# Reordering attention around the first feed-forward phases of a fused attention and feed-forward kernel on one core

## The chip, the core and the metric

The kernel runs on one core of one Trainium2 chip. The metric is the device time of one execution in microseconds (us); lower is better. Times are told as the median of several runs. A profile of one execution has its own span, from the first to the last instruction.

The engines named here: TensorE (PE in the profile, its weight loads PEld) multiplies matrices into the eight banks of PSUM; VectorE (DVE) and ScalarE (ACT) work on tensors; GpSimd (POOL) here only issues loads, and SyncE (SP) only issues stores and a few small loads. A suffix q (SPq, ACTq) stands for an instruction of an engine's queue, such as issuing a DMA.

## The reference

Eight batches of eight heads, 512 local and 32 global positions of 64 numbers a head:

```python
s_g = scale * np.matmul(q_g, k_all.transpose(0, 1, 3, 2))
out_g = np.matmul(sm(s_g), v_all)
mask = np.abs(pos[:, None] - pos[None, :]) <= 32
s_ll = np.where(mask, scale * np.matmul(q_l, k_l.transpose(0, 1, 3, 2)), -1e9)
s_lg = scale * np.matmul(q_l, k_g.transpose(0, 1, 3, 2))
out_l = np.matmul(sm(np.concatenate([s_lg, s_ll], -1)), np.concatenate([v_g, v_l], 2))
...
x = attn_out.transpose(0, 2, 1, 3).reshape(B * S, H * D)      # 4352 x 512
h = x @ w_in                                                  # 512 -> 2048
return (h * (1 / (1 + np.exp(-1.702 * h)))) @ w_out           # 2048 -> 512
```

So global queries look at everything, local queries at the global keys and a band of 32 to each side, and the result goes through a feed-forward layer with a quick GELU. The inputs are float32; the kernel multiplies in bf16.

## The kernel before, in words

**Attention, by quads.** A `Quad` is four heads of one batch, so each batch has two, called `a` and `c` in the code, and quads 0 to 15 follow each other. The four heads lie on the four groups of 32 partitions. A quad goes through these steps:

- `Tk`, `Tq` (together `T`, L254 to L268): VectorE turns keys and queries, 128x512 each; `ext` (L270): four small copies put the global queries beside the local ones. `transpose_g` (L208) turns the global queries and keys of a batch.
- `S(rnd)` (L277): TensorE makes the scores of one half (round 0 or 1) of the key chunks, 16 matmuls for the four heads into four banks of PSUM (`s4`, one buffer). A score tile has two chunks of columns beside each other, 228 and 200 wide (200 and 228 in round 0). Quad 0's second half goes to four single banks instead.
- `X(rnd)` (L314): ScalarE takes the exponential of the whole tile in one instruction, 128x1712, or bank by bank for quad 0's second half. `M(rnd)` (L325): VectorE multiplies by the band mask, 128x1408.
- `gg` and `K` (L350, L330): scores of global keys; `XK` (L354) their exponential; `eg` (L336) a block-diagonal copy.
- `ekU(unit)` (L358) and `U(unit)` (L378): TensorE adds, in one bank per unit (`ov`), the part of the global keys and that of the local keys: unit 0 is the sums of the softmax, units 1 and 2 are the two halves of the values. `UG` and `ekUs` call these in order.
- `R` (L408): VectorE turns the sums, takes the reciprocal and turns it back; `XL(0)`, `XL(1)` (L418) scale units 1 and 2 into `xL`, the input of the feed-forward layer. `Gm` (L393) and `G` (L421) do the same for the global queries (the result goes to `xG`).

**Feed-forward, by batches.** For each batch i, an h phase of 16 steps (`h_step`, L466): four matmuls of 512 columns into one bank (`hp`), ScalarE's tanh (L462) and VectorE's product (L463) into `gT`. Then an o phase: four tiles of 128 rows, each of four o steps (`o_mm`, L473) of four matmuls; the last step of a tile calls `o_out` (L485): ScalarE copies the bank to `ob`, and four stores go out, issued by SyncE. The global rows of all batches are one more pass at the end (i = B); its last tile is computed by columns in two parts, each with its own copy and stores.

**What sets the order.** Each engine does its instructions in the order in which the Python code issues them; that order is written out by hand. Attention of batch i + 1 is placed inside the o phase of batch i (`phase_o`, L672) and, for the first quad of it, near the end of the phase before. The first phases are written out step by step: quads 0 and 1 at L511 to L589, the h phase of batch 0 at L591, its o phase with quads 2 and 3 at L608 to L650 (`osteps(0, (tile, quarter), ...)` are its o steps), and the h phase of batch 1 at L655 to L670, with the preparation of quad 4, the first of batch 2, put in after certain steps. Waits between engines are set by the framework from the tiles that an instruction reads and writes. The four banks of the pool `psP` are shared by `hp`, `op`, `ov`, `kb` and `og`, each taking one as it comes free.

**Loads.** GpSimd issues keys, queries, values and the weights in one fixed order (`load_rest`, L214): values of batch 0, four blocks of w_in, two of w_out, then the rest. Block 1 of w_in covers the first half of d_model for the first half of d_ff, block 2 the second half of d_model, blocks 3 and 4 the same for the other half of d_ff.

**Dummies.** `keep(n, ps)` (L160) issues n matmuls on a tile of zeros; 62 of them stand at the beginning, four more before the second scores of quad 0.

Of the kernel before, what the change touches and what calls it, by code (L numbers as in the profile page):

```python
# [15 lines left out]
AF = mybir.ActivationFunctionType  # L16
# [4 lines left out]
def kernel(  # L21
# [12 lines left out]
    nc = tc.nc  # L34
# [9 lines left out]
    scale = 1.0 / (D ** 0.5)  # L44
# [5 lines left out]
    LW = 352  # L50
    RW = 428
# [105 lines left out]
    warm = consts.tile([128, 512], BF16)  # L157
    nc.vector.memset(warm, 0.0)

    def keep(n, ps, w=512):  # L160
        for _ in range(n):
            nc.tensor.matmul(ps[:, :w], lhsT=warm[:, 0:128], rhs=warm[:, :w], start=True, stop=True)
# [12 lines left out]
    mask = consts.tile([128, 2, LW], BF16)  # L175
# [32 lines left out]
    def transpose_g(lo, hi, names="qk"):  # L208
        for name, dst, s in (("q", qgT, rqg), ("k", kgT, rkg)):
            if name not in names:  # L210
                continue
            nc.vector.transpose(dst[:, lo:hi, :32], s[:, lo:hi].bitcast(F32))
# [21 lines left out]
    def pbank(name):  # L234
        return psP.tile([128, 512], F32, name=name, tag="p")

    class Quad:
# [73 lines left out]
                                     rhs=rv[:, :, ee] if len(rv.shape) == 3 else rv[:, :, :, ee],  # L311
                                     start=(ee == 0), stop=(ee == 1), skip_group_check=True)

        def X(self, rnd):  # L314
            e = self.E[rnd]
            if isinstance(self.ps, list):
                for j in range(4):
                    n = RW + 32 if j == 2 else RW
                    nc.scalar.activation(e[:, j, :n], self.ps[j][:, :n], AF.Exp, scale=scale)  # L319
                return  # L320
            nc.scalar.activation(e[:, :, :RW], self.ps[:, :, :RW], AF.Exp, scale=scale)  # L321
            if rnd == self.gr:
                nc.scalar.activation(e[:, 2, RW:], self.ps[:, 2, RW : RW + 32], AF.Exp, scale=scale)

        def M(self, rnd):  # L325
            lo = 36 if rnd else 40
            e = self.E[rnd][:, :, lo : lo + LW]
            nc.vector.tensor_mul(e, e, mask[:, rnd : rnd + 1, :].to_broadcast([128, 4, LW]))  # L328

        def K(self, e=None):  # L330
            if e != 1:
# [23 lines left out]
            self.ek = att.tile([128, Sl], BF16, name="ek")  # L355
            nc.scalar.activation(self.ek, self.kb, AF.Exp, scale=scale)  # L356

        def ekU(self, unit):  # L358
            ov = self.st[unit] = pbank("ov")
            for j in range(4):  # L360
                r = 32 * ((j + 1) % 4)
                p = slice(r, r + 32)
                lv = (ones32[p] if unit == 0 else
                      rvg[p, self.Q, :D].rearrange("p (w h) -> p w h", h=2)[:, :, unit - 1])
                nc.tensor.matmul(ov[32 * j : 32 * j + 32, :], lhsT=lv, rhs=self.ek[p],  # L365
                                 start=True, stop=False, skip_group_check=True)
# [99 lines left out]
    def h_step(i, fc):  # L466
        if fc == 0:
            gTs[i] = moe.tile([128, FC, TB], BF16, name="gT")
        hp = pbank("hp")
        h_mm(i, fc, hp, range(NKC))  # L470
        h_act(i, fc, hp)

    def o_mm(i, st):  # L473
        tci, f4 = divmod(st, 4)
        first = (i, tci) not in ops
        if first:
            ops[i, tci] = pbank("op")
        op = ops[i, tci]
        for fc in range(4 * f4, 4 * f4 + 4):
            nc.tensor.matmul(op, lhsT=gTs[i][:, fc, tci * 128 : tci * 128 + 128],  # L480
                             rhs=w_out_sb[:, fc, :], start=(first and fc == 4 * f4), stop=(fc == FC - 1))
        if f4 == 3:
            o_out(i, tci, op)

    def o_out(i, tci, op):  # L485
        ob = moe.tile([128, d_model], F32, name="ob", bufs=6)
        last = i == B and tci == B // 4 - 1
        for lo, hi in ((0, 256), (256, 512)) if last else ((0, 512),):
            if last:
                op = pbank("op")  # L490
                for fc in range(FC):
                    nc.tensor.matmul(op[:, lo:hi], lhsT=gTs[i][:, fc, tci * 128 : tci * 128 + 128],  # L492
                                     rhs=w_out_sb[:, fc, lo:hi], start=(fc == 0), stop=(fc == FC - 1))
            nc.scalar.activation(ob[:, lo:hi], op[:, lo:hi], AF.Copy, scale=0.5)  # L494
            for j in range(4):
                eng = nc.scalar if lo and j % 2 else nc.sync
                if i < B:
                    rows = out[i * S + Sg : (i + 1) * S, :].rearrange("(r t) m -> t r m", t=16)[4 * tci + j]
                else:
                    r = (4 * tci + j) * S  # L500
                    rows = out[r : r + Sg, :]
                eng.dma_start(out=rows[:, lo:hi], in_=ob[32 * j : 32 * j + 32, lo:hi])
# [8 lines left out]
    a, c = Quad(0), Quad(1)  # L511
# [37 lines left out]
    c.K(0)  # L549
    a.ekU(0)  # L550
    c.K(1)
    a.ekU(1)
    a.ekU(2)
    c.XK()
    a.U(0)
    a.R()
    c.S(1)
    c.X(1)
    a.U(1)
    a.U(2)  # L560
    a.Gm()
    c.M(0)
    a.XL(0)
    c.M(1)
    a.XL(1)
    gTs[0] = moe.tile([128, FC, TB], BF16, name="gT")
    pt = pts[0] = psS.tile([128, 4, 512], F32, name="s4")
# [36 lines left out]
    def osteps(i, *sts):  # L604
        for tci, f4 in sts:
            o_mm(i, 4 * tci + f4)

    nq = {1: (Quad(2), Quad(3)), 2: (Quad(4), Quad(5))}  # L608
    a, c = nq[1]
    a.T()  # L610
    a.ext()
    osteps(0, (0, 1), (0, 0), (1, 1), (1, 0))
    c.ext()
    a.S(0)
    a.gg()
# [2 lines left out]
    a.XK()  # L618
    a.M(0)
    a.eg()  # L620
    osteps(0, (2, 1), (2, 0), (0, 2), (0, 3))
    a.S(1)
    a.X(1)
    c.T()
    a.M(1)
    osteps(0, (1, 2), (1, 3))
    osteps(0, (2, 2))
    c.S(0)
    osteps(0, (2, 3))
    a.ekUs(c)  # L630
    c.XK()
    c.X(0)
# [4 lines left out]
    a.U(2)  # L637
    c.S(1)
    a.Gm()
    a.XL(0)  # L640
    a.XL(1)
    a.G()
    c.M(0)
    c.eg()
    c.X(1)
    c.M(1)
    osteps(0, (3, 1), (3, 2))
    c.UG()
    c.RXG()
    osteps(0, (3, 3))  # L650
    a, c = nq[2]
# [2 lines left out]
    load_g(8, NQ)  # L654
    for fc in range(FC):  # L655
        h_step(1, fc)
        if fc == 3:
            a.T()
        if fc == 5:
            transpose_g(4, 6)  # L660
            a.ext()
        if fc == 7:
            a.S(0)
            a.gg()
            a.K()
            a.XK()
            a.X(0)
        if fc == 10:
            a.M(0)
            a.eg()  # L670

# [66 lines left out]
    for st in range(4):  # L738
        o_mm(B, st)
    o_out(B, 1, None)  # L740


# [28 lines left out]
```

## Time and profile before

| | |
|---|---|
| median of 6 runs | 315.32 us (314.39 to 316.2) |
| the profiled execution: its own time | 315.11 us |
| its span, first to last instruction | 313.4 us |
| TensorE busy | 299.0 us (95%) |
| VectorE busy | 210.8 us (67%) |
| ScalarE busy | 167.2 us (53%) |
| GpSimd busy | 80.0 us (26%) |
| first h matmul of batch 0 / of batch 1 | 19.8 us / 58.7 us |
| first scores after the h phase of batch 1 | 75.1 us |
| last o matmul ends / last store is issued | 309.5 us / 310.7 us |

A row of the timeline has the start in us, the duration in us, the engine, the line of the kernel, the operation, output and inputs with their sizes, the count, and in brackets how long the engine had been idle and what ended that. A row with a count above 1 covers several instructions in a row. Busy time of TensorE overlaps from one matmul to the next, so the duration of one matmul is longer than the spacing between two.

### The profile page before, as it was taken

Reading aid. Unit: us, or ns where it says so; the run is one execution under the profiler, and the core shown is the slowest. Engines: PE = TensorE matmul, PEld = TensorE weight load, DVE = VectorE, ACT = ScalarE, POOL = GpSimd, SP = SyncE. Lnnn points to the kernel's source line nnn. Section 1 sums busy time; section 2 is a strip of 40 time slices with the busy share of each in tenths; the row PEclk is TensorE's granted clock in tenths of the full one; section 3 lists DMA queues with packets and bytes.
Section 4 is the critical chain, followed back from the end, with each engine's and each line's share of the span. In section 5 each row is a group of like instructions: output and inputs, shape, how many; then the busy total and the mean of one; then the engine's idle time right before and its main releaser. Section 6 shows DMA issues by size and latency. Waiting matters only on the chain.

```text
span 313.4 us, 7832 instructions
## 1 busy us (share of the span) xinstructions
PE 299.0 (95%) x3214; PEld 148.6 (47%) x3250; DVE 210.8 (67%) x462; ACT 167.2 (53%) x253; POOL 80.0 (26%) x131
## 2 busy tenths in 40 slices
PE   7779999989999999999999999999999999999994
PEld 7334444434454454544554454444454444446653
DVE  7887945869767766777867866776857865474320
ACT  4816565366455654566536744565456642563421
POOL 8821578787018000720036000300000000000000
PEclk9999999999999999999999999999999999999999
DMA  7999999999939411990259212900211012201122
GB/s 155 146 189 207 207 137 198 179 160 147 93 72 167 68 27 44 118 152 2 46 83 168 46 36 64 108 0 19 52 41 30 0 38 50 52 0 28 41 64 71
DMA packets 60099, 27.44 MB, mean 88 GB/s; under 512 B 43296, under 2 KB 51744, under 8 KB 60064
## 3 DMA queue, kind: packets, MB, share of 16 engines
q0 software_dynamic: 51536, 17.11, 50.4%
q1 hardware_dynamic: 8000, 9.18, 12.0%
q10 hardware_dynamic: 528, 0.66, 0.6%
q8 instruction: 25, 0.41, 0.5%
q14 instruction: 10, 0.08, 0.1%
HBM read 35.13 MB, written 8.91 MB: 141 GB/s over the span
## 4 chain that ended last, share of the span: by engine, by line
PE 82%; DVE 5%; DMA 4%; POOL 4%; issue 2%; ACT 2%; DVEq 0%; POOLq 0%; ACTq 0%
PE op L480 35%; PE hp L455 31%; PE s L291 5%; PE ov L387 4%; DMA w_in_sb<-in_moe_w_in_dram 4%; PE ov L365 2%; POOL rk L84 2%; DVE gT L463 1%; PE op L492 1%; POOL v L97 1%; DVE e L328 1%; PE kb L310 1%; ACT th L462 1%; DMA rk<-in_k_l_dram 1%; DVE xL L419 1%
## 5 line engine op out<-in xcount | busy, mean ns | idle before, releaser
L480 PE MATMUL op<-w_out_sb,gT 128*128 128x512 bf16 x503 | 119.8, 380 | 1.8 <-issue 0.8
L463 DVE SCALAR_TENSOR_TENSOR gT<-th,hp 128x512 bf16<-128x512 f32 (+1 forms) x140 | 91.2, 656 | 43.1 <-ACT th L462 42.5
L455 PE MATMUL hp<-xL,w_in_sb 128*128 128x512 bf16 x487 | 108.1, 379 | 0.8 <-DVE gT L463 0.2
L462 ACT ACTIVATE th<-hp 128x512 f32<-128x512 f32 (+1 forms) x140 | 79.9, 573 | 43.5 <-PE hp L455 39.9
L455 PEld LDWEIGHTS <-w_in_sb 128*128 128x128 bf16 x576 | 56.1, 98 | 66.5 <-DMA w_in_sb<-in_moe_w_in_dram 1.6
L480 PEld LDWEIGHTS <-gT 128*128 128x128 bf16 x528 | 49.1, 98 | 56.2 <-issue 3.5
L321 ACT ACTIVATE e<-s 128x1712 bf16<-128x1712 f32 x31 | 49.5, 1597 | 14.3 <-PE s L404 8.9
L494 ACT ACTIVATE ob<-op 128x512 f32<-128x512 f32 (+1 forms) x35 | 20.5, 585 | 64.5 <-PE op L480 62.0
L97 POOL DMA_DIRECT2D v<-in_v_l_dram x36 | 27.0, 760 | 99.3 <-PE s L404 93.0
L84 POOL DMA_DIRECT2D rk<-in_k_l_dram x64 | 34.8, 553 | 11.9 <-DMA w_in_sb<-in_moe_w_in_dram 5.8
L410 DVE STREAM_TRANSPOSE sT<-ov 128x512 f32<-128x512 f32 x16 | 11.5, 717 | 33.1 <-PE ov L387 33.1
L328 DVE TENSOR_TENSOR e<-e,mask 128x1408 bf16<-128x1408 bf16 x32 | 28.0, 874 | 5.8 <-ACT e L321 5.5
L291 PE MATMUL s<-q,kT 32*128 32x200 bf16 (+1 forms) x512 | 21.3, 284 | 2.4 <-DVE q L273 0.7
L419 DVE TENSOR_TENSOR xL<-ov,rs 128x512 bf16<-128x512 f32 x32 | 20.7, 686 | 1.5
L291 PEld LDWEIGHTS <-kT 32*128 32x128 bf16 x512 | 11.1, 95 | 15.5 <-issue 10.0
L387 PE MATMUL ov<-e,v 128*32 128x192 bf16 (+1 forms) x512 | 13.1, 239 | 0.8 <-DMA v<-in_v_l_dram 0.8
L356 ACT ACTIVATE ek<-kb 128x512 bf16<-128x512 f32 x16 | 9.6, 600 | 8.1 <-PE kb L310 8.0
L414 DVE STREAM_TRANSPOSE rs<-rT 128x512 f32<-128x512 f32 x16 | 11.4, 712 | 0.6
L260 DVE STREAM_TRANSPOSE kT<-rk 128x512 f32<-128x512 f32 (+1 forms) x17 | 11.4, 673 | 0.2 <-DMA rk<-in_k_l_dram 0.2
L263 DVE STREAM_TRANSPOSE q<-rq 128x512 f32<-128x512 f32 (+1 forms) x17 | 10.9, 645 | 0.6 <-DMA rq<-in_q_l_dram 0.6
L387 PEld LDWEIGHTS <-v 128*32 128x32 bf16 x512 | 9.8, 96 | 2.9 <-issue 2.9
L310 PE MATMUL kb<-q,kgT 32*32 32x512 bf16 x128 | 10.0, 385 | 0.5 <-ACT e L319 0.5
(70 smaller groups left out, 153.5 us busy)
## 6 DMA issues: line engine op xcount, KB each, us to landing
out_dram<-ob SPq DMA_DIRECT2D x132, 64.0 KB, 1.8
rk<-in_k_l_dram POOLq DMA_DIRECT2D x64, 64.0 KB, 3.9
v<-in_v_l_dram POOLq DMA_DIRECT2D x28, 128.0 KB, 4.3
rq<-in_q_l_dram POOLq DMA_DIRECT2D x6, 512.0 KB, 6.9
w_in_sb<-in_moe_w_in_dram POOLq DMA_DIRECT2D x4, 512.0 KB, 12.6
w_out_sb<-in_moe_w_out_dram POOLq DMA_DIRECT2D x4, 512.0 KB, 13.8
rq<-in_q_l_dram POOLq DMA_DIRECT2D x3, 256.0 KB, 8.0
q<-in_q_l_dram ACTq DMA_DIRECT2D x1, 512.0 KB, 4.7
```

The source lines that it names most:

```text
L84: nc.gpsimd.dma_start(out=loaded[b][0][32 * j : 32 * j + 32, u], in_=kf[b, j][:, u])
L97: nc.gpsimd.dma_start(out=vtiles[b % 2][p, s, :, :, :D], in_=vf[b, t][:, hs])
L291: nc.tensor.matmul(ps[j][:, off : off + n * nr], lhsT=self.k[p, 128 * c : 128 * c + 128, e], rhs=self.q[p, t0 : t0 + n, r0 : r0 + nr, e], ...
L321: nc.scalar.activation(e[:, :, :RW], self.ps[:, :, :RW], AF.Exp, scale=scale)
L328: nc.vector.tensor_mul(e, e, mask[:, rnd : rnd + 1, :].to_broadcast([128, 4, LW]))
L387: nc.tensor.matmul(ov[32 * j : 32 * j + 32, :].rearrange("p (t r) -> p t r", t=16)[:, :, r0 : r0 + nr], lhsT=lv, rhs=self.E[c // 2][:, j, ...
L419: nc.vector.tensor_mul(self.x[:, 2 * self.u + h, :], self.st[1 + h], self.st["rs"])
L455: nc.tensor.matmul(hp[:, : width(i)], lhsT=w_in_c[:, fc // 8, kc, fc % 8 // 2, :, fc % 2], rhs=(xL[i] if i < B else xG)[:, kc, :], start=( ...
L462: nc.scalar.activation(th[:, :n], hp[:, :n], AF.Tanh, scale=0.851)
L463: nc.vector.scalar_tensor_tensor(gTs[i][:, fc, :n], in0=th[:, :n], scalar=1.0, in1=hp[:, :n], op0=ALU.add, op1=ALU.mult)
L480: nc.tensor.matmul(op, lhsT=gTs[i][:, fc, tci * 128 : tci * 128 + 128], rhs=w_out_sb[:, fc, :], start=(first and fc == 4 * f4), stop=(fc = ...
L494: nc.scalar.activation(ob[:, lo:hi], op[:, lo:hi], AF.Copy, scale=0.5)
```

## The change

The diff touches six places.

1. `ekU` gets dummies of its own: before it adds the part of the global keys, it can issue `warm` matmuls on zeros into its bank. In quad 0, units 1 and 2 of it move behind the sums and their transposes, with 3 and 4 dummies; unit 2 comes after the second scores of quad 1.
2. The second exponential of quad 1 (the last scores of batch 0) is done in two pieces, one per chunk of keys, and its mask in two pieces as well (192 and 160 columns a head).
3. In the o phase of batch 0, the o step (2, 1) moves ahead of quad 2's scores, and (2, 3) ahead of quad 3's.
4. In the same phase, VectorE's steps of quads 2 and 3 are ordered anew: quad 3's first mask ahead of quad 2's scaling, its second mask next, then `eg`, and quad 2's globals (`G`) last.
5. In the h phase of batch 1, the preparation of quad 4 is spread: keys turned after step 2 and queries after step 5 (before: both after 3), globals turned and copied after step 7 (before 5), scores, exponentials after step 9 (before 7), mask after step 12 (before 10).
6. The last tile of all is split into 320 and 192 columns instead of 256 and 256, and of each part's four stores two are issued by SyncE and two by ScalarE (before: all four of the first part by SyncE).

```diff
-        def X(self, rnd):
+        def X(self, rnd, halves=False):
...
-            nc.scalar.activation(e[:, :, :RW], self.ps[:, :, :RW], AF.Exp, scale=scale)
+            for lo, hi in ((0, 228), (228, RW)) if halves else ((0, RW),):
+                nc.scalar.activation(e[:, :, lo:hi], self.ps[:, :, lo:hi], AF.Exp, scale=scale)
...
-        def M(self, rnd):
-            lo = 36 if rnd else 40
-            e = self.E[rnd][:, :, lo : lo + LW]
-            nc.vector.tensor_mul(e, e, mask[:, rnd : rnd + 1, :].to_broadcast([128, 4, LW]))
+        def M(self, rnd, lo=0, hi=LW):
+            at = 36 if rnd else 40
+            e = self.E[rnd][:, :, at + lo : at + hi]
+            nc.vector.tensor_mul(e, e, mask[:, rnd : rnd + 1, lo:hi].to_broadcast([128, 4, hi - lo]))
...
-        def ekU(self, unit):
+        def ekU(self, unit, warm=0):
             ov = self.st[unit] = pbank("ov")
+            keep(warm, ov)
...
-        for lo, hi in ((0, 256), (256, 512)) if last else ((0, 512),):
+        for lo, hi in ((0, 320), (320, 512)) if last else ((0, 512),):
...
-                eng = nc.scalar if lo and j % 2 else nc.sync
+                eng = nc.scalar if last and j % 2 else nc.sync
...
     a.ekU(0)
     c.K(1)
-    a.ekU(1)
-    a.ekU(2)
     c.XK()
     a.U(0)
     a.R()
+    a.ekU(1, 3)
     c.S(1)
-    c.X(1)
+    c.X(1, halves=True)
+    a.ekU(2, 4)
     a.U(1)
...
     a.XL(0)
-    c.M(1)
+    c.M(1, 0, 192)
+    c.M(1, 192)
     a.XL(1)
...
-    osteps(0, (0, 1), (0, 0), (1, 1), (1, 0))
+    osteps(0, (0, 1), (0, 0), (1, 1), (1, 0), (2, 1))
...
-    osteps(0, (2, 1), (2, 0), (0, 2), (0, 3))
+    osteps(0, (2, 0), (0, 2), (0, 3))
...
-    osteps(0, (2, 2))
+    osteps(0, (2, 2), (2, 3))
     c.S(0)
-    osteps(0, (2, 3))
...
     a.Gm()
+    c.M(0)
     a.XL(0)
     a.XL(1)
-    a.G()
-    c.M(0)
-    c.eg()
     c.X(1)
     c.M(1)
+    c.eg()
+    a.G()
...
         h_step(1, fc)
-        if fc == 3:
-            a.T()
+        if fc == 2:
+            a.Tk()
         if fc == 5:
+            a.Tq()
+        if fc == 7:
             transpose_g(4, 6)
             a.ext()
-        if fc == 7:
+        if fc == 9:
             a.S(0)
...
-        if fc == 10:
+        if fc == 12:
             a.M(0)
             a.eg()
```

## The prediction

> **What bounds the kernel now.** I read the page first: TensorE 299.0 us busy of a span of 313.4, VectorE 210.8, ScalarE 167.2, so TensorE carries the time and only its idle stretches can be won. The view of waits, for TensorE alone, says where they are (engine, operation and line, who ended the wait: total us, times, longest).
>
> ```profile
> PE s L455 <- DMA w_in_sb<-in_moe_w_in_dram: 1.1, 1, 1.1
> PE ov L387 <- DVE e L328: 1.1, 2, 0.6
> PE ov L387 <- DMA v<-in_v_l_dram: 0.8, 1, 0.8
> PE s L291 <- DVE q L273: 0.7, 1, 0.7
> PE hp L455 <- DVE gT L463: 0.2, 1, 0.2
> ```
>
> All of these lie before 75 us; from there TensorE has no wait of note until the end, and the diff changes nothing between 76 and 303 us. So there are four places to cost: the first quads (to 23 us), the o phase of batch 0 (35 to 58.7), the h phase of batch 1 (58.7 to 75), and the last rows (from 303). The chain of the first 30 us (start, us, what) says what the first place hangs on.
>
> ```profile
> 11.09 11.50 DMA w_in_sb<-in_moe_w_in_dram
> 22.58 0.05 issue
> 22.63 1.90 PE s L455 x8
> ```
>
> The second block of w_in lands at 22.6 us, and the first h matmuls of the second half of d_model wait for it. The timeline of VectorE says how much the attention has in hand there: the last scaling of quad 1 (L419, two in 1.29 us from 20.13) ends at 21.42, 1.2 us before the weights. Behind it the margin stays small: the fourth block lands when GpSimd goes on at 28.63, and TensorE reaches those columns at about 28.7.
>
> For the other three places, the timeline (start, us, engine, what, count, idle before):
>
> ```profile
> 53.83 0.85 DVE L328 TENSOR_TENSOR e<-e,mask 128x1408 bf16<-128x1408 bf16 x1
> 54.73 0.89 DVE L328 TENSOR_TENSOR e<-e,mask 128x1408 bf16<-128x1408 bf16 x1
> 55.67 0.34 PE L387 MATMUL ov<-e,ones 128*32 128x192 bf16 x8 [0.60 <-DVE e L328]
> 56.05 0.72 DVE L410 STREAM_TRANSPOSE sT<-ov 128x512 f32<-128x512 f32 x1 [0.43 <-PE ov L387]
> 57.91 1.29 DVE L419 TENSOR_TENSOR xL<-ov,rs 128x512 bf16<-128x512 f32 x2
> 66.43 0.67 PE L291 MATMUL s<-q,kT 32*128 32x200 bf16 x16 [0.71 <-DVE q L273]
> 74.14 1.02 PE L455 MATMUL hp<-xL,w_in_sb 128*128 128x512 bf16 x4 [0.20 <-DVE gT L463]
> 309.90 0.82 ACTq L502 DMA_DIRECT2D out_dram<-ob  x2
> 310.71 0.42 SPq L502 DMA_DIRECT2D out_dram<-ob  x1
> ```
>
> The first five are one chain: masks, sums of quad 3, transposes, scaling; h of batch 1 starts at 58.66, when the first scaling is done. The next two are batch 2's preparation inside that h phase. The last two: SyncE issues its last store 0.4 us after ScalarE's last (310.3).
>
> **First quads.** Added: 7 matmuls of 512 columns on zeros. In steady runs one costs 216 ns (14 in 3.0 us of the o phases), so 1.5 us on TensorE. The two rank-32 products they precede (8 matmuls, about 0.43 us) move behind the sums of quad 0. So these sums start at 12.85 instead of 13.26 (the mask they need ends at 12.89), and the transposes of quad 0 at 13.40 instead of 13.81. Then 3 dummies and 4 products run to about 14.35, where the scores of quad 1 stood at 14.25 anyway, waiting for their bank until ScalarE ended at 14.20: 0.1 late. The 4 dummies (0.86) and 4 products end at 16.2, and the values matmuls of quad 0, which waited for v until 15.74, start 0.45 late. Behind them on TensorE's queue are quad 0's globals and all of quad 1; VectorE waits for them with the scaling at 16.28, now 16.7. The exp by halves: 128x1712 takes 1597 ns and 128x512 600, so 175 ns fixed and 0.83 ns a column; two passes of 912 and 800 cost 175 ns more. In the built order of the changed kernel the first half waits for the last score matmul, so it starts no sooner; it ends near 16.7, before VectorE comes to the mask at 17.35. The mask in two pieces costs about 0.05 more (a 1408-wide one 0.88, a 128-wide one 0.21). Sum: quad 1's last scaling ends near 21.9 instead of 21.42. The weights land at 22.6. **Zero**, with 0.7 us of cover left of 1.2; past that, each us costs one. A gain is excluded to 0.1, since the weights are issued by 13.2 us in an unchanged order.
>
> Nor can the dummies buy TensorE a faster clock: every 512-wide matmul after the opening lasted 376 to 394 ns, none of them longer.
>
> **O phase of batch 0.** One o step (4 matmuls, 0.86 us) moves ahead of quad 2's scores and one ahead of quad 3's. The first delays quad 2's scores from 38.83 to 39.7 and its exp with them, but TensorE then has 12 matmuls left where it had 16, and meets quad 2's second scores at 43.6 as before; ScalarE and VectorE idled there (2.9 and 1.9 us), and the w_out blocks needed at 41.8 and 42.7 are in by 38.8 and 41.3. The second removes a change between kinds of work and lets the third o tile leave its bank by 48.5; before, a product waited for that bank until 49.22. Quad 3's scores to sums take 1.39 us in the steady phases (79.26 to 80.65), so the sums start at 49.16, not 49.55: 0.4. Of it 0.2 reach quad 3's second scores (the o step between waits for its bank until 49.75) and their exp, 52.18 to 53.78.
>
> VectorE's new order is mask, scaling twice, mask, eg, globals. Transposes end at 51.44, mask to 52.25, scaling to 53.55, second mask 53.83 to 54.72 (was to 55.62). The sums' wait of 0.60 is gone: they end 0.83 sooner. But the globals of quad 2 (0.76, from 53.15 to the next start) now sit between mask and transposes: from 54.85 to 55.6. So the next transposes start at 55.6, not 56.05: what is late next is VectorE itself. **Gain 0.5** (0 if the globals come out later, 0.8 if they were free), and h starts at 58.2.
>
> **H phase of batch 1.** The same VectorE work: two transposes 1.24, small ones and copies about 0.75. An h step takes TensorE 0.864 (4 x 216) and VectorE about 0.62 back to back, so 0.25 a step is there to work off a lag. Before: both transposes after step 3, the copies after step 5, scores after step 7: copies at 66.20, scores at 66.43, 0.71 late. After (times of before): one transpose at 62.68, caught up by step 5; one at 65.26, caught up at step 7; small transposes 67.08, copies 67.35, scores 67.58. TensorE is through step 9 at 67.4, so it waits 0.2, not 0.71. ScalarE's block (2.4 us: 0.60 + 1.60 + 0.19) now starts after step 9: its next tanh is at 71.0, the gelus that TensorE needs for the banks of steps 14 and 15 end at 72.3 and 72.9, and it comes for them at 72.5 and 73.4. The wait of 0.20 goes too. **Gain 0.75** (0.3 to 1.0). Next in line: the last gelu ends near 76.5 (before 76.9), the transposes and copies of quad 5 at 78.15, and TensorE wants them at 78.2: just in time.
>
> **Last rows.** Columns 320 + 192 instead of 256 + 256. The 256-wide matmul runs at 110 ns (32 in 3.51), the 512-wide at 216, so 136 and 83: 16 x (136 + 83) = 3.51, the same. Here the Trainium skill speaks against the change ("TensorE: Matmul & The Clock Gate", section LDWEIGHTS (loading the stationary operand)): by its P/1.2, loading 128 columns takes 107 ns, more than 83, which would make the second part 16 x 107 = 1.71 instead of 1.33, 0.38 late. But the 62 opening pairs of load and 128-wide matmul ran at 92 ns (5.72 us), with most of them at the slow rate (314 ns each, later ones 219). So 107 isn't a floor here, and I take 83 (by 92 it would cost 0.14). The stores: SyncE had six, now four, and ScalarE two more at 308.5, in its idle time. SyncE's issues follow each other at 0.47, so its last starts at 310.3 rather than 310.71. **Gain 0.4** (0 to 0.5); beyond it ScalarE's own last store sets the end.
>
> **Sum.** 0 + 0.5 + 0.75 + 0.4 = 1.65. The profiled execution took 315.11 (span 313.4): 313.46. The median of the six runs is 0.21 above it, so 313.7. About 0.3% (0.95 us) is what a measurement of this kernel can tell from no change.
>
> **Rivals.**
> - Handed on: the globals in front of the transposes eat the o gain (0), and the h phase keeps half (0.4) with the stores 0.4: -0.8, 314.5. For: VectorE has little idle time from 50 to 60; against: sums wait 0.43 us for VectorE's input in any case. Chance 0.22.
> - More: ends of all costs, o 0.8, h 1.0, stores 0.5: -2.3, 313.0. For: the idle sits on the chain; against: the globals. Chance 0.10.
> - Slower: the end of the h phase is crowded. ScalarE's block of 2.4 us stands six steps before the end, not eight; with 0.26 a step (0.864 - 0.60) it works off 1.6, not 2.1, and mask and eg (1.0) come three steps before the end. If nothing of the block is absorbed, quad 5's scores wait 2.4 us behind their copies: 313.7 + 2.4 = 316.1. It decides from 1.65 us on. For: the cover there is nil; against: four banks, and scores and 16 o matmuls that don't need VectorE (4.15 us in the steady phases, 109.52 to 113.67). Chance 0.06.
> - The first quads run past the weights (not what the edit says): more than 0.7 us late, 1 us costs 1: 314.7. Chance 0.06.
>
> **Numbers.** The forecast holds 0.56. Low 312.8 and high 315.1 take in both ends of the costs (-2.4, -0.3). Faster by over 0.3%: the forecast nearly whole, "more", a third of "handed on": 0.70. Within: 0.23. Slower: 0.07.
>
> **What would show it.** First h matmuls of the second half still at 22.6 behind the DMA; the 0.60 wait at the sums gone and the next transposes right behind the globals; h of batch 1 starting near 58.2 and ending 1.2 to 1.3 us sooner; scores after step 9 waiting 0.2; last SyncE store at 0.4 less after the last copy. Wrong if h of batch 0 starts later, if quad 5's scores wait for VectorE, or if idle time appears after 76 us.

## The result and the profile after

The changed kernel takes 313.38 us (median of 34 runs, 312.4 to 316.26) where the kernel before takes 315.3 (71 runs, 314.09 to 317.88). The ratio is 0.9948, with an interval of 0.9935 to 0.9961: 1.6 us less, by 1.2 to 2.1. The profiled execution took 312.8 us, with a span of 311.1 (before: 315.11 and 313.4). The forecast of 313.7 is 0.3 above the median. The sum was right to that, its terms less so.

I split both profiled executions at four instants that can be read off TensorE's and ScalarE's timelines. Every kernel below is laid into this table again, in us:

| stretch | before | after | forecast | measured |
|---|---|---|---|---|
| start of the span to the first o matmul of batch 0 | 35.12 | 34.82 | 0 | see below |
| from there to the first h matmul of batch 1 | 23.54 | 22.68 | -0.5 | -0.86 |
| from there to quad 4's second scores | 16.44 | 15.51 | -0.75 | -0.93 |
| from there to the last tile's first matmul | 230.70 | 230.70 | 0 | 0 |
| the last tile, to the end of its last copy | 4.07 | 4.07 | 0 | 0 |
| from there to the end of the span | 3.53 | 3.32 | -0.4 | -0.21 |

The 230 us that the diff leaves alone agree to 0.01, and no idle time appears in them. So what is won early is not given back later. The two middle stretches brought 1.79 where 1.25 was forecast, the stores half of theirs.

TensorE's waits after (what it waited for: us in total, times, longest; "w" is the wait for the first dummies at the start of both kernels):

```profile
PE w L162 <- DVE warm L158: 1.5, 1, 1.5
PE s L291 <- DVE kT L260: 1.4, 1, 1.4
PE s L291 <- DVE q L263: 0.8, 1, 0.8
PE op L482 <- issue: 0.6, 4, 0.2
PE kb L310 <- ACT e L319: 0.5, 1, 0.5
PE hp L457 <- DVE xL L421: 0.3, 1, 0.3
PE ov L389 <- DVE e L329: 0.2, 1, 0.2
```

The wait for w_in is gone, and so is that for v. The waits for the masks (L329) fell from 1.1 to 0.2: 0.60 of it in the o phase is gone, and 0.54 in the first quads became 0.20. The 0.7 for quad 4's copies (L273) has left the list, which shows waits over 0.15 only; 0.13 of it is left. The two rows for kT and q are the opening, and the edits begin behind both. The wait for kT is longer than before (0.7) because the opening dummies were done sooner in this execution, at 6.54 against 7.19; the scores begin at 7.90 in both. The queries did come later (0.4 before). One new row stands there, 0.3 for `xL` at the first h matmul of batch 1.

VectorE at the end of the o phase of batch 0, after (start, duration, work):

```profile
53.31 0.89 DVE L329 TENSOR_TENSOR e<-e,mask 128x1408 bf16<-128x1408 bf16 x1 [0.35 <-ACT e L322]
54.12 0.22 DVE L339 TENSOR_TENSOR eg<-bd,e 128x128 bf16<-128x128 bf16 x1
54.25 0.16 DVE L426 RECIPROCAL rg<-og 128x1 f32<-128x1 f32 x1
54.45 0.28 DVE L428 TENSOR_SCALAR xg<-og,rg 128x64 bf16<-128x64 f32 x1
54.77 0.24 DVE L429 STREAM_TRANSPOSE xG<-xg 128x64 bf16<-128x64 bf16 x1
54.94 0.68 DVE L412 STREAM_TRANSPOSE sT<-ov 128x512 f32<-128x512 f32 x1
56.75 1.29 DVE L421 TENSOR_TENSOR xL<-ov,rs 128x512 bf16<-128x512 f32 x2
```

TensorE there and in the h phase after it:

```profile
57.50 1.24 PE L457 MATMUL hp<-xL,w_in_sb 128*128 128x512 bf16 x5 [0.29 <-DVE xL L421]
...
64.83 1.46 PE L457 MATMUL hp<-xL,w_in_sb 128*128 128x512 bf16 x6
66.42 0.67 PE L291 MATMUL s<-q,kT 32*128 32x200 bf16 x16
...
73.01 0.67 PE L291 MATMUL s<-q,kT 32*128 32x228 bf16 x16
```

The mask is followed by `eg`, the globals and the transposes with no bracket between them: VectorE works from 53.31 to the scaling without a pause, and TensorE comes for the first scaling 0.29 before it is done. The mask that ended at 55.62 before now ends at 54.20. Before h of batch 1 at 57.50 there are 22.68 us to the first o matmul, not 23.54. Quad 4's scores come at 66.42, after 0.13 of idle time.

### The profile page after: what moved, and what is told of

Its sections match the earlier page's. It is cut to its first block, busy times and chain, and to the rows that moved or that the text cites. A ratio compares the mean times of both kernels' runs of the same rounds, so it can differ in the third digit from the quotient of the medians.

```text
span 311.1 us, 7848 instructions
## 1 busy us (share of the span) xinstructions
PE 299.6 (96%) x3220; PEld 148.1 (48%) x3257; DVE 210.6 (68%) x463; ACT 167.2 (54%) x254; POOL 79.9 (26%) x131
## 4 chain that ended last, share of the span: by engine, by line
PE 79%; DMA 10%; POOL 5%; DVE 2%; issue 1%; ACT 1%; ACTq 0%; POOLq 0%; DVEq 0%
PE op L482 33%; PE hp L457 32%; DMA w_out_sb<-in_moe_w_out_dram 9%; PE s L291 5%; PE ov L389 4%; POOL v L97 2%; PE ov L367 2%; POOL rk L84 2%; DMA rk<-in_k_l_dram 1%; POOL w_in_sb L219 1%; PE op L494 1%; PE kb L310 1%; DVE gT L465 1%; PE s L406 1%; PE s L310 1%
## 5 line engine op out<-in xcount | busy, mean ns | idle before, releaser
L322 ACT ACTIVATE e<-s 128x1712 bf16<-128x1712 f32 (+2 forms) x32 | 49.6, 1552 | 15.7 <-PE s L406 8.9
L496 ACT ACTIVATE ob<-op 128x512 f32<-128x512 f32 (+2 forms) x35 | 20.5, 585 | 61.6 <-PE op L482 59.1
L329 DVE TENSOR_TENSOR e<-e,mask 128x1408 bf16<-128x1408 bf16 (+2 forms) x33 | 28.0, 851 | 6.0 <-ACT e L322 6.0
L291 PE MATMUL s<-q,kT 32*128 32x200 bf16 (+1 forms) x512 | 21.3, 284 | 2.3 <-DVE kT L260 1.4
```

The lines of the kernel that those rows point to most:

```text
L291: nc.tensor.matmul(ps[j][:, off : off + n * nr], lhsT=self.k[p, 128 * c : 128 * c + 128, e], rhs=self.q[p, t0 : t0 + n, r0 : r0 + nr, e], ...
L322: nc.scalar.activation(e[:, :, lo:hi], self.ps[:, :, lo:hi], AF.Exp, scale=scale)
L329: nc.vector.tensor_mul(e, e, mask[:, rnd : rnd + 1, lo:hi].to_broadcast([128, 4, hi - lo]))
```

## The experiments

The diffs are against the kernel before for the first four, and against the changed kernel from then on where nothing else is said. Ratios are to the kernel before, timed on the same chip.

**One part alone, four kernels.**

The first has only edits 1 and 2: the products of quad 0 moved with their 7 dummies, exponential and mask of quad 1 in two pieces.

> The kernel before with only the edits of the first quads (dummies, moved products, exp and mask in two pieces). Theory: the second block of w_in sets when h of batch 0 goes on, so the time is the same within 0.3 us, quad 1's last scaling ends 0.5 to 1.1 us later than 21.4 and the matmuls still follow the weights at 22.3 to 22.7. Rival: the edits themselves give the 0.3 us by which the changed kernel's profile has its o phase start sooner; then the time falls by 0.3. A third: the cover is used up and the time rises by up to 0.5.

The second has only edits 3 and 4, the o steps and VectorE's order in the o phase of batch 0.

> The kernel before with only the new order in the o phase of batch 0. Theory as predicted: 0.5 us faster, limited by the globals in front of the transposes. Rival, from the changed kernel's profile: 0.85 us faster, since the phase from its start to the first h matmul of batch 1 shrank by that much there. A second rival: nothing, since the h phase behind it waits for its own preparation (scores of quad 4 wait longer by what is won).

The third has only edit 5, the preparation in the h phase of batch 1.

> The kernel before with only the preparation of quad 4 spread in the h phase of batch 1. Theory: 0.75 to 0.95 us faster, the waits of 0.71 and 0.20 gone, and none behind them. Rival: half of it is handed on as a wait of quad 5's scores for VectorE, 0.4 us faster.

The fourth has only edit 6, the last tile's columns and stores.

> The kernel before with only the last tile's new split (320 and 192 columns) and stores shared by SyncE and ScalarE. Theory as predicted: 0.4 us faster, SyncE's last store issued 0.4 sooner after the last matmul. Rival, from the changed kernel's profile: 0.2 us, since ScalarE's last store is issued no sooner than before and ends the span.

| kernel | time | ratio | o phase | h phase | last tile | after it |
|---|---|---|---|---|---|---|
| edits 1, 2 | 314.92 | 1.0024 [1.0002, 1.0046] | 23.53 | 16.44 | 4.08 | 3.56 |
| edits 3, 4 | 313.78 | 0.9969 [0.9948, 0.9990] | 22.68 | 16.45 | 4.07 | 3.51 |
| edit 5 | 313.82 | 0.9971 [0.9957, 0.9986] | 23.53 | 15.52 | 4.07 | 3.51 |
| edit 6 | 314.49 | 0.9992 [0.9975, 1.0010] | 23.53 | 16.44 | 4.45 | 3.34 |

(The span is read to 0.1, so the last column is good to about 0.05.) Edits 3 to 5 each move their own stretch and no later one, by the same amount as in the changed kernel. For them alone or together makes no difference, so the two mechanisms don't feed one another. The rival "handed on", by which the globals eat the o gain, has fallen: the o phase alone gives 0.86 in the profile and 0.0031 x 315 = 1.0 in the times. Edits 1 and 2 alone are slower, just measurably.

Edit 6 alone gained nothing, and its row shows why. ScalarE in the last tile, with edit 6 alone:

```profile
307.38 0.44 ACT L494 ACTIVATE ob<-op 128x320 f32<-128x320 f32 x1 [1.58 <-PE op L492]
307.85 1.23 ACTq L502 DMA_DIRECT2D out_dram<-ob  x2
309.13 0.33 ACT L494 ACTIVATE ob<-op 128x192 f32<-128x192 f32 x1 [1.31 <-PE op L492]
```

And in the changed kernel:

```profile
306.08 0.44 ACT L496 ACTIVATE ob<-op 128x320 f32<-128x320 f32 x1 [1.58 <-PE op L494]
306.55 0.85 ACTq L504 DMA_DIRECT2D out_dram<-ob  x2
307.45 0.33 ACT L496 ACTIVATE ob<-op 128x192 f32<-128x192 f32 x1 [0.93 <-PE op L494]
307.81 0.84 ACTq L504 DMA_DIRECT2D out_dram<-ob  x2
...
308.22 0.43 ACTq L504 DMA_DIRECT2D out_dram<-ob  x1
308.27 0.31 SPq L504 DMA_DIRECT2D out_dram<-ob  x1
```

(The last two rows are from a narrower window of the same view.) Two stores on ScalarE's queue take 0.85, or 1.23 when one of them is held up. They stand between the two copies, so in the second case the last copy is 0.38 late and the gain of 0.2 is gone. The same happened once more, in the kernel with `eg` earlier, below (1.21, last tile 4.42): in 2 of the 10 profiles with edit 6. What holds the store up I didn't test by itself, and it stays open. It is not a store that uses the same semaphore and has not landed: with edit 6 alone the last one to do so was issued at 302.73 and took 1.7 to land, so it was down more than 3 us before. The traces do show a companion. In both profiles an instruction load of 8 KB (queue q14) falls into the part, 0.56 behind the first copy's end, and the stores of the first part take 1.9 to 2.1 to land, where the changed kernel's take 1.5 to 1.7. But in two other profiles (changed without edits 1 and 2, and the first kernel of the last table below) the load falls there too, and no store is held up.

**The first quads taken out, and their dummies doubled.** The changed kernel without edits 1 and 2:

> The changed kernel with the first quads as in the kernel before (edits 1 and 2 undone), all else as changed. Compared with the changed kernel (ratio 0.9948 to before). Theory: quad 1's last scaling and the second block of w_in arrive together with the edits, up to 1 us apart without them, so undoing them gives 0 to 0.7 us: ratio 0.992 to 0.995, and the profile shows matmuls that wait for the DMA again. Rival: the edits gained 0.3; then the ratio is 0.996.

and with twice the dummies:

```diff
-    a.ekU(1, 3)
+    a.ekU(1, 6)
...
-    a.ekU(2, 4)
+    a.ekU(2, 8)
```

> The changed kernel with 6 and 8 dummies in place of 3 and 4 (1.5 us more matmuls on zeros). Theory from the profiles: the cover of the first quads is used up by the change itself, since its last scaling ends with the landing of w_in, so all 1.5 us reach the end: ratio to before near 0.9995. Rival, as predicted: 0.7 us of cover is left, and 0.8 us reach the end: ratio 0.9975.

Without the edits 312.94 us, ratio 0.9940 [0.9912, 0.9969]; doubled 314.14, ratio 0.9968 [0.9952, 0.9985]. The doubled kernel's last scaling of quad 1:

```profile
22.71 1.29 DVE L421 TENSOR_TENSOR xL<-ov,rs 128x512 bf16<-128x512 f32 x2
```

In the changed kernel this row starts at 21.24. So 7 more dummies (1.5 us at 216 ns) move the scaling by 1.47, and the first o matmul moves by the same, from 34.82 to 36.29. In these two executions no cover is left to take any of it. The times show less. The ratio is 0.0020 above the changed kernel's, and 0.0030 above that of the kernel with the last tile in halves (below), which was timed beside it: 0.6 to 0.9 us, not 1.5. So by the times the theory of the expectation (0.9995) missed, and its rival (0.9975) lies within the interval. What takes up the rest isn't shown. Executions in which the weights land late could do it, and so could the clock drops below, which no timed run of the doubled kernel had.

All fourteen profiled executions, sorted by this, give a rule without exceptions. "Scores" is the start of quad 1's first scores, which wait for its queries to land. "Scaling" is the end of the row above. "Weights" is when GpSimd goes on because the second block of w_in has landed. The columns in us:

| kernel | scores | scaling | weights | first o matmul |
|---|---|---|---|---|
| before | 11.81 | 21.42 | 22.87 | 35.12 = weights + 12.25 |
| edits 3, 4 | 11.81 | 21.57 | 22.76 | 35.00 = weights + 12.24 |
| edit 5 | 11.81 | 21.39 | 22.63 | 34.88 = weights + 12.25 |
| edit 6 | 12.29 | 21.83 | 22.10 | 34.35 = weights + 12.25 |
| no edits 1, 2 | 11.83 | 21.48 | 22.46 | 34.70 = weights + 12.24 |
| edits 1, 2 | 11.81 | 22.11 | 22.15 | 34.40 = scaling + 12.29 |
| after | 12.22 | 22.53 | 22.52 | 34.82 = scaling + 12.29 |
| after, again | 12.08 | 22.38 | 21.28 | 34.67 = scaling + 12.29 |
| last tile in halves | 12.68 | 22.98 | 21.96 | 35.26 = scaling + 12.28 |
| dummies doubled | 12.18 | 24.00 | 22.02 | 36.29 = scaling + 12.29 |

(Of the four others, described below, the two without edits 1 and 2 follow the first law, at 12.25 each, and the two with them the second, at 12.29 each.) From scores to scaling it takes 9.5 to 9.8 us without the edits and 10.30 with them: 0.70 more, and the same in every profile but the doubled kernel's and one with a lowered clock (below). The inputs land differently from one execution to the next: the weights between 21.3 and 22.9, the queries so that the scores start between 11.8 and 12.9. In the profiles without the edits the weights are always last, with 0.3 to 1.5 us of cover. With them attention is last, or level with the weights. What the edits cost is at most their own delay, 0.70. By the table it is nothing for "edits 1, 2" (34.40 by either law), and the whole 0.70 for "after, again": there attention would have ended at 21.68 without them, still behind the weights at 21.28.

**No dummies, order kept.** To tell the dummies from the rest of edits 1 and 2:

```diff
-    a.ekU(1, 3)
+    a.ekU(1)
...
-    a.ekU(2, 4)
+    a.ekU(2)
```

> The changed kernel with its 7 dummies taken out, the products still moved behind the sums. Theory: the dummies are what delays quad 1's last scaling by 0.7 us, so it ends near 21.5 again (21.9 where quad 1's queries land 0.4 later), TensorE waits for w_in, and the time is 0 to 0.3 us less than the changed kernel's. Rival: the moved products or the two-piece exp and mask carry the delay; then the scaling stays near 22.1 to 22.5. Second rival: without dummies a clock falls and matmuls last longer.

313.12 us, ratio 0.9938 [0.9920, 0.9957], timed beside the changed kernel once more, unedited:

> The changed kernel once more, beside the three below and the kernel before. Theory: ratio to before near 0.995, and its stages (first o step to h of batch 1, h to quad 4's second scores) 22.68 and 15.51 us as before.

which gave 313.33, 0.9951 [0.9925, 0.9976]. The two can't be told apart. In the profile the scaling ends 9.95 behind the scores, against 10.30 with the dummies and about 9.6 without edits 1 and 2, although the clock was low in it. So the dummies carry at least 0.35 of the 0.70, and how the rest divides isn't shown. The same execution showed what dummies may be for. Its stretches of 1 us (busy us and counts of each engine, then the granted clock of TensorE, DMA share and GB/s):

```profile
11.00:12.00 1.00, 0.40 (x16) 0.28 (x9) 0.13 (x1) 1.00 (x4) 1.00 (x3) 1.00 2.27 158
12.00:13.00 1.00, 0.07 (x4) 0.07 (x7) 0.83 (x2) 0.45 (x1) 1.00 (x2) 1.00 2.61 148
13.00:14.00 1.00, 1.00 (x28) 0.40 (x27) 0.82 (x5) 0.36 (x1) 0.89 (x2) 0.84 2.33 159
14.00:15.00 1.00, 1.00 (x28) 0.43 (x16) 0.00 (x0) 1.00 (x1) 0.22 (x1) 0.50 1.35 168
15.00:16.00 1.00, 1.00 (x20) 0.40 (x16) 0.72 (x2) 0.82 (x3) 0.98 (x2) 0.50 1.02 130
16.00:17.00 1.00, 1.00 (x20) 0.26 (x8) 0.97 (x3) 0.38 (x1) 0.62 (x2) 0.50 0.98 150
17.00:18.00 1.00, 1.00 (x60) 0.91 (x56) 1.00 (x2) 1.00 (x2) 0.00 (x0) 0.95 1.06 193
```

and the matmuls in it:

```profile
12.93 0.67 PE L291 MATMUL s<-q,kT 32*128 32x200 bf16 x16 [1.53 <-DVE q L263]
...
14.41 0.78 PE L389 MATMUL ov<-e,ones 128*32 128x160 bf16 x16
15.12 0.61 PE L367 MATMUL ov<-ek,rvg 32*32 32x512 bf16 x4
15.67 0.90 PE L291 MATMUL s<-q,kT 32*128 32x228 bf16 x16
```

The queries came late, TensorE was idle for 1.53 us, and 0.8 us after it had resumed the granted clock fell to 0.50 and stayed there for 3.4 us (by the 0.84 and 0.95 of the slices at its ends, from 13.7 to 17.1). In the 3.4 us before the drop TensorE had been busy for 1.43. The sums took 0.78 instead of 0.49, the scores 0.90 instead of 0.67.

The runs carry a mean clock too, and 3.4 us at half speed take 1.7 / 312 = 0.005 off it. (The clock also falls to half when the work is done, here from 310.6 on, so that the mean of this execution is 0.993. No run has 0.996.) So I counted runs with a mean below 0.997. Kernels without the change's dummies: 44 of 167. With them: 19 of 75. Doubled: 0 of 12. For the changed kernel (47 runs of both its labels) the median of such runs is 315.01 and of the others 313.12; for the kernel before (90 runs on the chips of the experiments) 315.44 and 314.76. So nothing shows that the seven dummies make the drop rarer. Where it happens it costs the changed kernel more (1.9 against 0.7); that the dummies do this, by running at half speed too, is argued, not shown. Twelve runs of the doubled kernel without one are a hint (at one in four, none in 12 would come 3 times in 100) that 14 dummies are enough, but at 314.14 they seem to cost more than they save. Where in those runs the clock fell isn't recorded; only one drop was caught in a profile.

**The h phase: is it the spread or the delay?** The transposes put back to where they stood before, scores and mask left two steps later:

```diff
-        if fc == 2:
-            a.Tk()
+        if fc == 3:
+            a.T()
         if fc == 5:
-            a.Tq()
-        if fc == 7:
             transpose_g(4, 6)
```

> The changed kernel with quad 4's transposes together after step 3 and the global ones after step 5, as before, and only the scores after step 9 and the mask after step 12. Theory: what removes the 0.71 us wait is that the scores come two steps later, so the time equals that of the changed kernel within 0.2 us. Rival: the transposes must be spread, or VectorE's lag of 1.3 us shows as a wait for a bank at steps 6 to 8: 0.3 to 0.6 us slower than the changed kernel.

312.79 us, ratio 0.9921 [0.9894, 0.9948], and the h phase takes 15.31 instead of 15.51. VectorE in it, this kernel:

```profile
62.13 0.70 DVE L260 STREAM_TRANSPOSE kT<-rk 128x512 f32<-128x512 f32 x1
...
62.76 0.67 DVE L263 STREAM_TRANSPOSE q<-rq 128x512 f32<-128x512 f32 x1
63.35 1.25 DVE L465 SCALAR_TENSOR_TENSOR gT<-th,hp 128x512 bf16<-128x512 f32 x2
...
64.80 0.58 DVE L273 COPY q<-qgT 128x40 f32<-128x40 f32 x4
```

and in the changed kernel:

```profile
64.13 0.70 DVE L263 STREAM_TRANSPOSE q<-rq 128x512 f32<-128x512 f32 x1
64.75 1.25 DVE L465 SCALAR_TENSOR_TENSOR gT<-th,hp 128x512 bf16<-128x512 f32 x2
...
66.20 0.76 DVE L273 COPY q<-qgT 128x40 f32<-128x40 f32 x4
```

With the transposes left where they were, the copies are done by 65.4, and the scores start at 65.97 behind step 9 with no wait. Spread, the copies start at 66.20, and the scores come behind them. The two transposes of 0.7 cost TensorE nothing when they stand together: no idle time of it shows before the scores (the program gives it four banks to work ahead in). So the gain is the delay of the scores, and the spread takes 0.2 of it back. In two of the seven profiles with the spread it was more: 15.83, where the scores waited 0.44 and 0.45. There the copies start where they do in the other five, 8.7 behind the first h matmul, but the first of them, for which the scores wait, takes 0.47 and 0.49 instead of 0.17. Why is open. In the kernel without the spread the first copy took 0.55, and it cost nothing, since it had started 1.17 before the scores.

**The last tile in halves**, to test the rule on weight loads:

```diff
-        for lo, hi in ((0, 320), (320, 512)) if last else ((0, 512),):
+        for lo, hi in ((0, 256), (256, 512)) if last else ((0, 512),):
```

> The changed kernel with the last tile split into 256 and 256 columns again, its stores still shared by SyncE and ScalarE. Theory: the split itself is worth nothing on TensorE (3.5 us both ways) and 0.05 on the last copy, so the time equals that of the changed kernel within 0.1 us. Rival: loading weights bounds the 192-wide matmuls, and 256 and 256 is 0.2 to 0.4 us faster. Another: ScalarE's two stores of the first part now stand closer in front of the last copy and delay it by up to 0.4.

313.26 us, ratio 0.9938 [0.9913, 0.9963]; last tile 4.08 against 4.07. The split is worth nothing, as forecast. The matmuls of the tile, in the changed kernel and in this one:

```profile
303.71 3.66 PE L494 MATMUL op<-w_out_sb,gT 128*128 128x320 bf16 x32
304.14 3.66 PE L494 MATMUL op<-w_out_sb,gT 128*128 128x256 bf16 x32
```

**The best of it, and `eg` moved.** Edits 3, 4 and 6, with the scores and masks of edit 5 but not its spread, and without edits 1 and 2. Against the kernel before, the h phase is only

```diff
-        if fc == 7:
+        if fc == 9:
             a.S(0)
...
-        if fc == 10:
+        if fc == 12:
             a.M(0)
```

> The kernel before with the new order of the o phase, the last tile's edits, and in the h phase only the scores after step 9 and the mask after step 12 (transposes as before; first quads as before). Theory: the stages are 22.68 and 15.31 us, so 0.2 us less than the changed kernel from the h phase and 0 to 0.3 from the first quads: ratio to before 0.993. Rival: the spread transposes and the first quads' edits don't matter, ratio 0.995.

The last one has besides, against this,

```diff
     a.XL(1)
+    c.eg()
     c.X(1)
     c.M(1)
-    c.eg()
     a.G()
```

> e10 with quad 3's eg moved ahead of its second exp, into VectorE's idle 0.35 us before the second mask. Theory: VectorE's chain (mask, globals, transposes, scaling) sets the start of h of batch 1, so that stage shrinks by 0.13 us to 22.55, and the wait of 0.28 at the first h matmul to 0.15. Rival: another wait takes its place and the stage stays 22.68. In the timed runs 0.13 us can't be told from nothing.

| kernel | time | ratio | o phase | h phase | last tile | after it |
|---|---|---|---|---|---|---|
| edits 1, 2 out, no spread | 312.66 | 0.9924 [0.9895, 0.9953] | 22.68 | 15.31 | 4.08 | 3.31 |
| the same, `eg` earlier | 312.99 | 0.9925 [0.9900, 0.9950] | 22.54 | 15.31 | 4.42 | 3.36 |
| the changed kernel again | 313.33 | 0.9951 [0.9925, 0.9976] | 22.67 | 15.83 | 4.07 | 3.27 |

The first is the best kernel here by its stretches: 0.2 less in the h phase than the changed kernel's first profile, and at its start the weights are last again. In the times its 0.7 us below the changed kernel are within the intervals. Moving `eg` into VectorE's gap takes 0.14 off the o phase:

```profile
53.12 0.21 DVE L338 TENSOR_TENSOR eg<-bd,e 128x128 bf16<-128x128 bf16 x1
53.57 0.89 DVE L328 TENSOR_TENSOR e<-e,mask 128x1408 bf16<-128x1408 bf16 x1 [0.24 <-ACT e L321]
54.38 0.16 DVE L424 RECIPROCAL rg<-og 128x1 f32<-128x1 f32 x1
...
55.06 0.67 DVE L410 STREAM_TRANSPOSE sT<-ov 128x512 f32<-128x512 f32 x1
```

The mask is followed directly by the globals, and the transposes come 1.49 behind the mask's start instead of 1.63 (54.94 - 53.31). That shows that VectorE's own row of work sets the start of h. The late store, 0.35 in this execution, took it back.

## Why the prediction was right, step by step

**First quads, forecast 0: failed as to its size.** "0.7 us of cover left of 1.2" was taken from one execution in which the queries landed early and the weights late. The cover ranges from 0.3 to 1.5. The delay was 0.70, not 0.48. One part of it: quad 1's second scores come 2.66 behind its first instead of 2.44, that is 0.22 late where I had 0.1, and the first scaling of quad 0, 5.10 behind those first scores instead of 4.47, is 0.63 late where I had 0.42. The halved exponential was cheaper than reckoned, 1.66 for both pieces instead of 1.60 (I had added 0.175). By the table above the step costs 0 to 0.7. Timed alone it cost 0.0024 x 315 = 0.8 (0.1 to 1.4); among the runs with a mean clock of 0.997 and more the medians, 314.67 and 314.50, differ by 0.2. The sentence "past that, each us costs one" held to 0.01 in the profile of the doubled kernel, and by its times only for about half.

**O phase, forecast -0.5: right in mechanism, 0.35 too small.** The chain went as written: the wait at the sums is gone, the globals are what is late next, and VectorE sets h (0.29 in TensorE's row, and the `eg` kernel). The term that was mis-sized is the start of the globals. From the first o matmul, the globals start at 54.25 - 34.82 = 19.43, where the forecast had 54.85 - 35.12 = 19.73. Of these 0.3, about 0.1 is that `eg` begins 0.08 before the mask's row ends, and 0.2 that quad 3's mask was ready earlier: 53.31 - 34.82 = 18.49 instead of 53.83 - 35.12 = 18.71. That mask waits for the exponential of quad 3's second scores, and those follow the sums of quad 2. Before, then after:

```profile
49.55 0.49 PE L387 MATMUL ov<-e,ones 128*32 128x160 bf16 x16
51.66 0.67 PE L291 MATMUL s<-q,kT 32*128 32x228 bf16 x16
...
48.69 0.49 PE L389 MATMUL ov<-e,ones 128*32 128x160 bf16 x16
50.96 0.67 PE L291 MATMUL s<-q,kT 32*128 32x228 bf16 x16
```

From the first o matmul the sums came 0.56 sooner (14.43 to 13.87), where I had 0.4, and the scores 0.40 sooner (16.54 to 16.14), where I had 0.2. The 0.2 that I had charged for a bank did come, as 0.16. The remaining 0.06 is a misreading. I took the globals for 0.76, but that is up to the end of their last piece; the row before,

```profile
53.15 0.16 DVE L424 RECIPROCAL rg<-og 128x1 f32<-128x1 f32 x1
```

is followed by the next work at 53.83, 0.68 later, and after the change they take 54.94 - 54.25 = 0.69.

**H phase, forecast -0.75: near in size (-0.93), the reason only half right.** What I took off the two waits adds up to 0.71 (0.51 and 0.20), not 0.75; why 0.93 came is not shown in full. I had the copies and the scores at step 9 wait for each other with 0.2 left over, and that is about what came: 0.13 of idle time, and a stretch 0.2 above that of the kernel without the spread. What I didn't ask was whether the spread is needed. The delay by two steps alone gives 1.13 (16.44 - 15.31).

**Last rows, forecast -0.4: 0.2.** SyncE's last store did come 0.35 sooner: 310.71 before is 0.84 behind the last copy's end (309.87), 308.27 after is 0.49 behind it (307.78). But ScalarE's second store starts 0.44 behind the copy's end, as before, and "beyond it ScalarE's own last store sets the end" is what happened: the end came 0.21 sooner. What I missed is the price of a store on ScalarE's queue between the two copies, 0.35 to 0.38 when it is held up. The rule of the Trainium skill that spoke against the split ("TensorE: Matmul & The Clock Gate", section LDWEIGHTS (loading the stationary operand)) did not decide. It gives the length of one load, 107 ns (the trace records 98); that pairs of load and matmul can't follow each other faster was my inference, and it failed. The 16 pairs of the second part, with 192 columns each, lie within the 1.37 between the two copies' starts (307.45 - 306.08), so a pair took at most 86 ns, and the tile's 32 matmuls take 3.66 with either split. By P/1.2 the part would have taken 1.71.

**The rivals.** "Handed on" and the crowded end of the h phase did not come: no wait for VectorE shows at quad 5's scores. "More" is where the middle stretches went. "The first quads run past the weights" did come, at 0 to 0.7 us an execution, and hides in the sum: 0.86 + 0.93 + 0.21 = 2.0 gained by the stretches, and 1.6 (1.2 to 2.1) by the times. The difference of 0.4 is of the size of that cost. So the forecast came out near partly because one term too small and one left out cancel.

**"Nor can the dummies buy TensorE a faster clock"** was wrong as an argument. The profile of before held no slow matmul because that execution had no drop. Twenty-seven of 90 runs of that kernel had a mean clock below 0.997. The dummies of the change still bought nothing, but that took the counts to see.

## What to carry to other kernels

A margin between a load and the work that it hides should be taken over several executions, not from the one that was profiled: here one load moved by 1.1 us and another by 1.6, as much as the margin or more. When a wait is cured by moving both its producer and its consumer, try the consumer alone. And before work is put on a queue that also does the next step of the critical chain, as the stores on ScalarE's queue, ask what it costs there if it is held up.

## What the runs showed of the hardware

The granted clock fell to half for 3.4 us in a stretch in which TensorE was idle for no more than 1.53 us at a time, and was busy for 1.43 of the 3.4 us before it. The drop came 0.8 us after TensorE had resumed. About one run in four of these kernels has a mean clock that fits one such stretch (0.992 to 0.995, with what falls at the end) or two (0.987 and 0.989).

Two stores issued by ScalarE in a row took 0.82 to 0.85 us, or 1.21 and 1.23 in two of ten profiles, and the copy behind them came 0.35 and 0.38 late.
